# Stage one of batches 1 to 3: the folded transform's two halves as two column tiles of the array, one copy per bank

## The chip, the cores and the metric

The kernel runs on one core of one Trainium2 chip. The metric is device time in microseconds of one execution. The time before is the median of three runs. All durations below come from one profiled execution of the kernel before.

## What is computed

A long convolution by FFT, gated with x, and then a feed-forward block with a squared ReLU, in single precision:

```python
def _attn_ref(x, v, pos_emb, w1, w2):          # x, v: 4 x 12480 x 128
    h_mlp = np.maximum(pos_emb @ w1, 0.0) @ w2
    h_filt = h_mlp * np.exp(-0.01 * np.arange(S))[:, None]
    u = x * v
    Uf = np.fft.rfft(u, n=2 * S, axis=1)
    Hf = np.fft.rfft(h_filt, n=2 * S, axis=0)
    y = np.fft.irfft(Uf * Hf[None], n=2 * S, axis=1)[:, :S, :]
    return x * y

def _moe_ref(x, w_in, w_out):                  # d_ff = 2048
    h = np.maximum(x @ w_in, 0.0)
    return h * h @ w_out
```

## The kernel before, in words

Each batch has 112 x 112 (padded) positions and 128 channels. Its FFT convolution goes through four stages, each a generator: `stage1` (transform along one index of the 112 x 112 grid), `stage2` (twiddles, second transform, product with the filter's spectrum `Hd`), `stage3` and `stage4` (the way back, and the product with x). The first batch's stages and the filter's run at the start of the kernel by themselves. After that the feed-forward block runs over 4 x 28 column groups `i` of 446 columns, each in 8 steps `f`. Between its pieces a step of that loop takes up the next pieces of the FFT stages of batches 1 to 3: `adv(1)`, `adv(2)` and `adv(3)` each run the generator chain up to its next `yield`. One feed-forward step so carries one iteration of the stage that is due: its loads and evacuation (1), its preparation (2) and its matmuls (3). The instructions of each engine are in the order in which Python emits them.

On TensorE a feed-forward step is twelve matmuls of 128 x 128 weights with 446 columns (lines 81 to 83: six into `A`, six into `O` or, late in the kernel, `F`). They are of type float32r. Stage one of batches 1 to 3 uses plain float32: `matmul` at line 297.

`stage1` with `big=False` has 32 iterations `t` (four channels each). `mul(t)` on GpSimd forms x times v, and from it `ut`: for each channel, 112 rows (the index that is summed over), columns 0 to 55 with the sum of two halves of the sequence, columns 56 to 63 zero, columns 64 to 119 with their difference. `mm(t)` takes two PSUM banks `A[h]` and for each of two channels `k` in a bank runs one matmul: `ut`'s 120 columns are the weights, the table `ef` (112 x 224, cosine and minus sine interleaved) streams through. Sums come out on PSUM partitions 0 to 55, differences on 64 to 119.

The difference rows need the table times -i: real and imaginary part exchanged, one of them negated. `evac(t, A)`, which runs one iteration later, does this on the way to `W`. For bank `h = 0`, ScalarE makes three instructions (line 316 for partitions 0 to 63, lines 317 and 318 for the two parts of partitions 64 to 119). For `h = 1`, VectorE makes two (line 309, and line 310 with the factors of the small tile `sign`). `ef` is loaded from `e_full` on the SP queue at the head of the stage, ahead of the first loads of x and v (lines 255 and 256); GpSimd writes `sign` by two memsets there.

The tag `F` has three PSUM banks. The matmul helper `mm3` (lines 81 to 83) is shared by all float32r matmuls.

Of the kernel before, what the change touches and what calls it, by code (L numbers as in the profile page):

```python
# [7 lines left out]
F32 = mybir.dt.float32  # L8
# [9 lines left out]
I = 112  # L18
# [12 lines left out]
HI = I // 2  # L31
KP = 64 + HI
# [3 lines left out]
def hyena_moe_kernel(  # L36
# [22 lines left out]
    nc = tc.nc  # L59
# [12 lines left out]
    def pool(name, side="left", **kw):  # L72
        return tc.tile_pool(name=name, bufs=kw.pop("bufs", 2), side=side, reuse_waits="tile", **kw)

    def bank():
        return psf.tile([128, 512], F32, tag="F", name="F")

    def mm3(o, L, R, first=True, last=True):
        lh, ll = L
        rh, rl = R  # L80
        nc.tensor.matmul(o, lh, rh, start=first, stop=False)  # L81
        nc.tensor.matmul(o, lh, rl, start=False, stop=False)  # L82
        nc.tensor.matmul(o, ll, rh, start=False, stop=last)  # L83
# [54 lines left out]
    def by_value():  # L138
        return W[:I].rearrange("p t (c d) -> p (t c) d", c=4)
# [4 lines left out]
    def first_rows():  # L144
        return W[:I].rearrange("p t (q d) -> p (t q) d", q=4)[:, :I].rearrange("p (e s) (c k) -> p c e s k", e=4, k=4)
# [77 lines left out]
    def rest(k):  # L223
        for _ in range(k):
            yield 1
            yield 2
            yield 3

    def stage1(b, big, et=None, side="left", hook=None):
        DC = 4  # L230
        n = D // DC
        with pool("s1", side) as p:
            if big:
                E = (et[:, 0, :], et[:, 1, :])
            else:
                ef = p.tile([I, 2 * I], F32, name="ef", bufs=1)
                nc.sync.dma_start(out=ef, in_=e_full)
                sign = p.tile([KP, 2], F32, name="sign", bufs=1)
                nc.gpsimd.memset(sign[:, 0:1], 1.0)
                nc.gpsimd.memset(sign[:, 1:2], -1.0)  # L240
            ext = 3 if big else 0
            pa = (3 if b is None else 2) if big else 1
            fold = not big
            J = KP if fold else I
            L = {}
            halves = [p.tile([I, DC, KP], F32, name=f"ut{k}", bufs=1) for k in range(3)] if fold else []
            for ut in halves:
                nc.gpsimd.memset(ut[:, :, HI:64], 0.0)

            def load(t):  # L250
                if b is None or t >= n:
                    return
                xt = p.tile([I, DC, I], F32, tag="xt", name="xt", bufs=2 + pa + ext)
                vt = p.tile([I, DC, I], F32, tag="vt", name="vt", bufs=2 + ext)
                nc.sync.dma_start(out=xt, in_=xs[b, :, t * DC : (t + 1) * DC, :])
                nc.sync.dma_start(out=vt, in_=vs[b, :, t * DC : (t + 1) * DC, :])
                L[t] = xt, vt

            def mul(t):
                if b is None or t >= n:  # L260
                    return
                xt, vt = L[t]
                eng = nc.vector if big and t in (0, 2, 4) else nc.gpsimd
                eng.tensor_mul(out=xt, in0=xt, in1=vt)
                if fold:
                    ut = halves[t % 3]
                    eng.tensor_add(out=ut[:, :, :HI], in0=xt[:, :, :HI], in1=xt[:, :, HI:])
                    eng.tensor_sub(out=ut[:, :, 64:], in0=xt[:, :, :HI], in1=xt[:, :, HI:])
                    L[t] = ut, None

            def like(x):
                return x if b is not None else x.rearrange("p d (s k) -> p d s k", k=4)

            def prep(t):
                if t >= n or fold:
                    return
                u = first_rows()[:, t] if b is None else L.pop(t)[0]
                hi = p.tile([I, DC, J], F32R, tag="uh", name="uh", bufs=1 + pa)
                nc.scalar.copy(like(hi), u)
                q[t] = u, hi  # L280

            def prep2(t):
                if t >= n or fold:
                    return
                u, hi = q[t]
                lo = p.tile([I, DC, J], F32R, tag="ul", name="ul", bufs=1 + pa)
                nc.vector.tensor_sub(out=like(lo), in0=u, in1=like(hi).bitcast(F32))
                q[t] = hi, lo

            def mm(t):  # L290
                hi, lo = (L.pop(t)[0], None) if fold else q.pop(t)
                A = []
                for h in range(DC // 2):
                    A.append(bank())
                    for k in range(2):
                        if fold:
                            nc.tensor.matmul(A[h][:J, k * 2 * I : (k + 1) * 2 * I], hi[:, 2 * h + k, :], ef, start=True, stop=True)  # L297
                            continue
                        mm3(A[h][:J, k * 2 * I : (k + 1) * 2 * I], (hi[:, 2 * h + k, :], lo[:, 2 * h + k, :]), E)
                return A  # L300

            def evac(t, A):
                for h in range(DC // 2):
                    d0 = t * DC + 2 * h
                    if fold:
                        view = W.rearrange("p t (k r d) -> p (t k) r d", k=2, r=2)[:, :, :, d0 : d0 + 2]
                        src = A[h][:KP, : 4 * I].rearrange("p (d c r) -> p c r d", d=2, r=2)
                        if h:
                            nc.vector.tensor_copy(view[:64], src[:64])
                            nc.vector.tensor_mul(  # L310
                                out=view[64:],
                                in0=src[64:, :, ::-1],
                                in1=sign[64:].rearrange("p (c r d) -> p c r d", c=1, d=1).to_broadcast([HI, I, 2, 2]),
                            )
                        else:
                            nc.scalar.copy(view[:64], src[:64])
                            nc.scalar.copy(view[64:, :, 0], src[64:, :, 1])
                            nc.scalar.mul(view[64:, :, 1], src[64:, :, 0], -1.0)
                        continue
                    dst = by_value()[:, :, d0 : d0 + 2]  # L320
                    src = A[h][:I, : 4 * I].rearrange("p (d t) -> p t d", d=2)
                    if big and h:
                        nc.vector.tensor_copy(dst, src)
                    else:
                        nc.scalar.copy(dst, src)

            q = {}
            la = 2 + pa + ext
            early = min(la, 2 + ext)
            for t in range(early):  # L330
                load(t)
            if big:
                yield 1
            else:
                yield from rest(2)
            for t in range(pa + 1):
                mul(t)
            for t in range(early, la):
                load(t)
            yield 1  # L340
            for t in range(pa):
                prep(t)
            yield 2
            for t in range(pa):
                prep2(t)
            prev = None
            for t in range(n):
                yield 1
                load(t + la)
                mul(t + pa + 1)  # L350
                if prev is not None:
                    evac(t - 1, prev)
                prep(t + pa)
                yield 2
                prep2(t + pa)
                yield 3
                prev = mm(t)
                if hook is not None:
                    hook(t - n)
            yield 1  # L360
            evac(n - 1, prev)
# [515 lines left out]
    for i in range(B * NG):  # L877
        for f in range(NS):
            adv(1)
            A = m_h(zT, f)  # L880
# [24 lines left out]
def _constants():  # L905
# [7 lines left out]
    def split(a):  # L913
        hi = r12(a)
        return hi, r12(a - hi.astype(np.float64))

    def split16(a):
        hi = a.astype(np.float16)
        return hi, (a - hi.astype(np.float64)).astype(np.float16)
# [2 lines left out]
    m = np.arange(NP)  # L922
    a = 2 * np.pi * ((4 * n[None] + 1) * n[:, None] % (4 * I)) / (4 * I)
    e = np.stack([np.cos(a), -np.sin(a)], 2).reshape(I, 2 * I)
    e_full = e.astype(np.float32)
    e_tab = np.stack(split(e), 1)

    def th(i):
# [7 lines left out]
    k = n[:, None] + I * n[None]  # L936
# [4 lines left out]
    c, s = split16(np.cos(ph)), split16(np.sin(ph))  # L941
    t2 = np.stack([c[0], s[0], c[1], s[1]], 2)
    ph = angle(2 * n - (I - 1))
    c, s = split16(np.cos(ph)), split16(np.sin(ph))
# [8 lines left out]
    c, s = split16(np.cos(ph)), split16(np.sin(ph))  # L953
# [69 lines left out]
```

## Time and profile before

| what | value |
|---|---|
| median of 3 runs | 3316.22 us (3314.28 to 3319.64) |
| the profiled execution's own time | 3318.15 us |
| its span, first to last instruction | 3316.4 us |
| mean granted TensorE clock | 0.994 of full speed |

The span is 1.75 us less than the profiled execution's time. In the rows below PE is TensorE's matmuls, PEld its weight loads, DVE VectorE, ACT ScalarE, POOL GpSimd, SP the queue that issues most transfers. One float32 `matmul` statement shows as two weight loads and two matmul records; a float32r one as one of each. A matmul record's duration reaches to its modelled end, so records of one engine overlap; the distance from start to start is the time that it occupies.

### The profile page before, as it was taken

To read this page: it belongs to the slowest core of one execution; us is meant where nothing else is said; L and a number is where in the kernel's file an instruction comes from. 1 tells how busy PE (TensorE), PEld (TensorE's weight loads), DVE (VectorE), ACT (ScalarE), POOL (GpSimd) and SP (SyncE) were. 2 spreads that over 40 slices of the span, in tenths; PEclk is the share of its full clock that TensorE was granted. 3 is DMA by queue.
4 is the path that set the end of the run, shared out by engine and by line. 5 is a ranking of instruction groups with operands and counts; after the bars stand their busy time and mean duration, and the time that the engine had idled before them with its cause. 6 is when DMAs were issued, how large, how long until landed. Compare 5 with 4: busy or idle time off the path is not lost.

```text
span 3316.4 us, 55144 instructions
## 1 busy us (share of the span) xinstructions
PE 3266.2 (98%) x18814; PEld 3046.0 (92%) x18814; DVE 2644.3 (80%) x3330; ACT 2571.5 (78%) x3577; POOL 1336.1 (40%) x1411
## 2 busy tenths in 40 slices
PE   8999999999999999999999999999999999999998
PEld 8987989999999999999999999999999999999998
DVE  7999888878876689888876689888876679877776
ACT  6665778777788878778788788778787878888886
POOL 2579046646710046656620056665630046300000
PEclk9999999999999999999999999999999999999999
DMA  2899156434410056533410046533420046300000
GB/s 80 255 261 256 59 135 156 129 94 121 121 35 18 22 129 158 134 100 112 121 45 18 18 117 157 132 111 107 122 62 12 17 101 158 93 26 24 25 23 20
DMA packets 338627, 321.65 MB, mean 97 GB/s; under 512 B 144873, under 2 KB 295273, under 8 KB 338345
## 3 DMA queue, kind: packets, MB, share of 16 engines
q1 hardware_dynamic: 307368, 260.90, 28.8%
q0 software_dynamic: 30976, 57.22, 7.4%
q8 instruction: 149, 2.44, 0.3%
q14 instruction: 134, 1.09, 0.1%
HBM read 226.53 MB, written 63.77 MB: 88 GB/s over the span
## 4 chain that ended last, share of the span: by engine, by line
PE 93%; DVE 2%; DMA 2%; issue 1%; ACT 1%; POOL 0%; SPq 0%; DVEq 0%; POOLq 0%; ACTq 0%
PE A L81 11%; PE A L83 11%; PE A L82 11%; PE F L81 9%; PE F L82 9%; PE O L82 9%; PE F L83 9%; PE O L83 9%; PE O L81 9%; PE F L297 4%; PE F L462 4%; DMA ht<-Hd 1%; DVE m L482 1%; DVE W L482 0%; DVE gl L822 0%
## 5 line engine op out<-in xcount | busy, mean ns | idle before, releaser
L803 ACT ACTIVATE r<-A 128x892 f32<-128x892 f32 x896 | 820.6, 916 | 302.1 <-PE A L83 284.9
L81 PE MATMUL A<-zh,wt 128*128 128x446 f32 x1792 | 702.0, 392 | 1.3 <-DVE gl L822 1.1
L822 DVE TENSOR_TENSOR gl<-r,gh 128x892 fp32r<-128x892 f32 x503 | 612.7, 1218 | 88.1 <-ACT r L810 74.5
L83 PE MATMUL A<-zh,wt 128*128 128x446 f32 x1792 | 653.5, 365 | 0.0
L82 PE MATMUL A<-zl,wt 128*128 128x446 f32 x1792 | 651.5, 364 | 0.0
L806 ACT ACTIVATE gh<-r 128x892 fp32r<-128x892 f32 x512 | 486.2, 950 | 142.6 <-PE O L83 131.2
L770 POOL TENSOR_TENSOR zl<-zi,zh 128x446 fp32r<-128x446 f32 x111 | 129.9, 1170 | 1150.8 <-PE F L83 600.9
L817 DVE CAST gh<-r 128x892 fp32r<-128x892 f32 x384 | 242.5, 631 | 359.2 <-ACT r L810 357.7
L82 PE MATMUL O<-gl,wt 128*128 128x446 f32 x1440 | 524.0, 364 | 1.5 <-DVE gl L822 1.3
L83 PE MATMUL O<-gh,wt 128*128 128x446 f32 x1440 | 524.2, 364 | 0.0
L81 PE MATMUL O<-gh,wt 128*128 128x446 f32 x1440 | 523.2, 363 | 0.0
L810 ACT ACTIVATE r<-r 128x892 f32<-128x892 f32 x504 | 479.3, 951 | 14.5
L822 DVE TENSOR_TENSOR gl<-A,gh 128x892 fp32r<-128x892 f32 x392 | 426.1, 1087 | 74.0 <-ACT gh L806 56.5
L808 DVE SCALAR_TENSOR_TENSOR A<-A,r 128x892 f32<-128x892 f32 x392 | 425.1, 1085 | 56.1 <-ACT r L803 53.9
L81 PEld LDWEIGHTS A<-zh,wt 128*128 128x128 f32 x1792 | 338.7, 189 | 26.9 <-DVE gl L822 2.4
L82 PEld LDWEIGHTS A<-zl,wt 128*128 128x128 f32 x1792 | 340.2, 190 | 19.8 <-DVE zl L770 0.2
L83 PEld LDWEIGHTS A<-zh,wt 128*128 128x128 f32 x1792 | 336.7, 188 | 22.8
L484 POOL TENSOR_TENSOR W<-W,m 112x256 f32<-112x256 f32 x224 | 230.9, 1031 | 206.4 <-DVE m L482 183.1
L621 POOL TENSOR_TENSOR al<-W,ah 112x512 fp32r<-112x512 f32 x212 | 278.7, 1315 | 47.2 <-ACT ah L619 34.2
L82 PEld LDWEIGHTS O<-gl,wt 128*128 128x128 f32 x1440 | 272.4, 189 | 22.5 <-DVE gl L822 3.3
L81 PEld LDWEIGHTS O<-gh,wt 128*128 128x128 f32 x1440 | 271.7, 189 | 18.8
L83 PEld LDWEIGHTS O<-gh,wt 128*128 128x128 f32 x1440 | 269.9, 187 | 18.2
(130 smaller groups left out, 6908.5 us busy)
## 6 DMA issues: line engine op xcount, KB each, us to landing
ht<-Hd SPq DMA_DIRECT2D x224, 224.0 KB
tb<-t POOLq DMA_DIRECT2D x224, 196.0 KB, 3.3
xt<-xs SPq DMA_DIRECT2D x128, 196.0 KB
vt<-vs SPq DMA_DIRECT2D x128, 196.0 KB
xt<-x SPq DMA_DIRECT2D x224, 112.0 KB
out<-ot SPq DMA_DIRECT2D x112, 223.0 KB
tb<-t2s SPq DMA_DIRECT2D x168, 105.0 KB
zd<-zs SPq DMA_DIRECT2D x222, 64.0 KB
```

The lines of the kernel that those rows point to most:

```text
L81: nc.tensor.matmul(o, lh, rh, start=first, stop=False)
L82: nc.tensor.matmul(o, lh, rl, start=False, stop=False)
L83: nc.tensor.matmul(o, ll, rh, start=False, stop=last)
L297: nc.tensor.matmul(A[h][:J, k * 2 * I : (k + 1) * 2 * I], hi[:, 2 * h + k, :], ef, start=True, stop=True)
L484: nc.gpsimd.tensor_sub(out=re[0], in0=re[0], in1=im[1])
L621: eng.tensor_sub(out=lo, in0=w, in1=hi.bitcast(F32))
L803: nc.scalar.activation(r, h, AF.Relu)
L806: nc.scalar.activation(hi, r, AF.Square)
L808: nc.vector.scalar_tensor_tensor(out=h, in0=h, scalar=0.0, in1=r, op0=ALU.max, op1=ALU.mult)
L810: nc.scalar.activation(r, r, AF.Square)
L817: nc.vector.tensor_copy(hi, g)
L822: nc.vector.tensor_sub(out=lo, in0=g, in1=hi.bitcast(F32))
```

## The change

The table gets a second half, -i times the first. Each matmul of 120 weight columns becomes two: the 64 columns of sums (with their zeros) with the first half into partitions 0 to 63, the 56 columns of differences with the second half into partitions 64 to 119. With exchange and sign already in the table, each bank is evacuated by one copy of 120 partitions: ScalarE for bank 0, VectorE for bank 1. The tile `sign` and its two memsets go.

```diff
-                ef = p.tile([I, 2 * I], F32, name="ef", bufs=1)
+                ef = p.tile([I, 2, 2 * I], F32, name="ef", bufs=1)
                 nc.sync.dma_start(out=ef, in_=e_full)
-                sign = p.tile([KP, 2], F32, name="sign", bufs=1)
-                nc.gpsimd.memset(sign[:, 0:1], 1.0)
-                nc.gpsimd.memset(sign[:, 1:2], -1.0)
...
                         if fold:
-                            nc.tensor.matmul(A[h][:J, k * 2 * I : (k + 1) * 2 * I], hi[:, 2 * h + k, :], ef, start=True, stop=True)
+                            o = A[h][:, k * 2 * I : (k + 1) * 2 * I]
+                            nc.tensor.matmul(o[:64], hi[:, 2 * h + k, :64], ef[:, 0, :], start=True, stop=True)
+                            nc.tensor.matmul(o[64:KP], hi[:, 2 * h + k, 64:], ef[:, 1, :], start=True, stop=True)
                             continue
...
                         src = A[h][:KP, : 4 * I].rearrange("p (d c r) -> p c r d", d=2, r=2)
-                        if h:
-                            nc.vector.tensor_copy(view[:64], src[:64])
-                            nc.vector.tensor_mul(
-                                out=view[64:],
-                                in0=src[64:, :, ::-1],
-                                in1=sign[64:].rearrange("p (c r d) -> p c r d", c=1, d=1).to_broadcast([HI, I, 2, 2]),
-                            )
-                        else:
-                            nc.scalar.copy(view[:64], src[:64])
-                            nc.scalar.copy(view[64:, :, 0], src[64:, :, 1])
-                            nc.scalar.mul(view[64:, :, 1], src[64:, :, 0], -1.0)
+                        (nc.vector.tensor_copy if h else nc.scalar.copy)(view[:KP], src)
                         continue
...
-    e_full = e.astype(np.float32)
+    e_full = np.stack([e, np.stack([-np.sin(a), -np.cos(a)], 2).reshape(I, 2 * I)], 1).astype(np.float32)
```

## Rows read from the trace of the kernel before

**Rows 1.** Page: engine, busy us (share of the span), instructions.

```profile
PE 3266.2 (98%) x18814; PEld 3046.0 (92%) x18814; DVE 2644.3 (80%) x3330; ACT 2571.5 (78%) x3577; POOL 1336.1 (40%) x1411
```

**Rows 2.** The chain that ended last, 600 to 740 us: shares, then start, us, what.

```profile
by line: PE F L297 34.8%; PE A L81 11.2%; PE A L83 11.0%; PE A L82 11.0%; PE O L83 10.8%; PE O L82 10.7%; PE O L81 10.7%; issue 0.0%
...
617.99 1.52 PE F L297 x8
...
633.80 1.51 PE F L297 x8
```

**Rows 3.** Busy time of each engine, batch 1's stage one: window, us, busy (instructions), clock, DMA.

```profile
609.82:737.60 127.78, 127.78 (x647) 120.69 (x648) 106.43 (x128) 98.49 (x170) 79.27 (x97) 1.00 0.37 110
```

**Rows 4.** Timeline of PE, 615 to 645 us: start, us, instructions merged where adjacent.

```profile
617.62 0.37 PE L83 MATMUL O<-gh,wt 128*128 128x446 f32 x1
617.82 1.68 PE L297 MATMUL F<-ef,ut 112*120 112x224 f32 x8
619.18 0.53 PE L81 MATMUL A<-zh,wt 128*128 128x446 f32 x1
619.54 0.37 PE L82 MATMUL A<-zl,wt 128*128 128x446 f32 x1
619.75 0.37 PE L83 MATMUL A<-zh,wt 128*128 128x446 f32 x1
...
621.79 1.68 PE L297 MATMUL F<-ef,ut 112*120 112x224 f32 x8
...
625.73 1.68 PE L297 MATMUL F<-ef,ut 112*120 112x224 f32 x8
```

**Rows 5.** Timeline of PEld, 617.5 to 619.6 us, same columns.

```profile
617.62 1.52 PEld L297 LDWEIGHTS F<-ef,ut 112*120 112x120 f32 x8
```

**Rows 6.** Groups by line, whole span: count, busy us, mean ns, idle before.

```profile
L81 PEld LDWEIGHTS A<-zh,wt 128*128 128x128 f32 x1792 | 338.7, 189 | 26.9 <-DVE gl L822 2.4 <-PE F L83 1.1 <-ACT r L803 1.0
...
L297 PE MATMUL F<-ef,ut 112*120 112x224 f32 x768 | 161.3, 352 | 0.0
...
L297 PEld LDWEIGHTS F<-ef,ut 112*120 112x120 f32 x768 | 140.2, 183 | 8.0 <-POOL ut L268 0.6
L462 PEld LDWEIGHTS F<-W,tb 120*112 120x112 f32 x672 | 117.6, 175 | 20.7
...
L310 DVE TENSOR_TENSOR W<-F,sign 56x448 f32<-56x448 f32 x96 | 60.4, 629 | 1.4
...
L309 DVE COPY W<-F 64x448 f32<-64x448 f32 x96 | 58.2, 606 | 0.0
...
L316 ACT COPY W<-F 64x448 f32<-64x448 f32 x96 | 51.8, 540 | 0.1
...
L323 DVE COPY W<-F 112x448 f32<-112x448 f32 x64 | 39.6, 620 | 5.9 <-PE F L83 3.5
...
L325 ACT COPY W<-F 112x448 f32<-112x448 f32 x64 | 36.1, 564 | 10.6 <-DVE W L323 6.4 <-PE F L83 3.9
L318 ACT ACTIVATE W<-F 56x224 f32<-56x224 f32 x96 | 35.3, 368 | 0.0
L317 ACT COPY W<-F 56x224 f32<-56x224 f32 x96 | 34.7, 362 | 1.1
```

**Rows 7.** Timeline of PE in stage three: first and last of twelve float32r pairs, next.

```profile
1001.78 0.27 PE L81 MATMUL F<-tab,vh 112*112 112x224 f32 x1
...
1002.93 0.27 PE L83 MATMUL F<-tab,vl 112*112 112x224 f32 x1
1003.04 0.37 PE L81 MATMUL A<-zh,wt 128*128 128x446 f32 x1
```

**Rows 8.** Who waited for whom, 609 to 738 us: total us, times, longest.

```profile
ACT r L803 <- PE A L83: 18.1, 33, 0.7
POOL ut L267 <- PE F L297: 16.1, 12, 1.6
...
PEld F L297 <- POOL ut L268: 0.4, 1, 0.4
```

**Rows 9.** Timeline of POOL at the head of batch 1's stage one.

```profile
602.50 0.10 POOL L239 MEMSET sign<- 120x1 f32 x1
...
607.23 1.16 POOL L264 TENSOR_TENSOR xt<-xt,vt 112x448 f32<-112x448 f32 x1 [4.43 <-DMA vt<-vs]
```

**Rows 10.** DMA issues: tile, queue, count, KB each; and GB/s in 40 slices.

```profile
GB/s 80 255 261 256 59 135 156 129 94 121 121 35 18 22 129 158 134 100 112 121 45 18 18 117 157 132 111 107 122 62 12 17 101 158 93 26 24 25 23 20
...
ef<-e_full SPq DMA_DIRECT2D x3, 98.0 KB
```

## The prediction

> **What bounds the kernel now.** I read the page's table of engines first: TensorE is busy for 98% of the span, VectorE 80%, ScalarE 78%, GpSimd 40% [rows 1]. That is an average, so the next view is the chain that ended last, cut to batch 1's stage one, where the change sits. There the chain is TensorE's matmuls and nothing else, and line 297 holds 34.8% of it, in pieces of 1.52 us per iteration [rows 2]. The busy times of the same stretch say the same: TensorE 127.78 of 127.78 us, at the full granted clock, with VectorE at 106 and ScalarE at 98 [rows 3]. The waits of the stretch confirm who is late: ScalarE waits for matmuls (18.1 us in all), GpSimd waits for line 297 to release `ut` (16.1 us); TensorE waited once, 0.4 us [rows 8]. So here a microsecond on TensorE is a microsecond of the kernel, and one taken from ScalarE or VectorE is worth nothing until TensorE waits for them.
>
> One iteration on TensorE: from one block of line 297 to the next 3.97 and 3.94 us [rows 4]. Twelve feed-forward matmuls take 0.20 each, 2.4 us; the rest is line 297's eight passes (four statements, two records each). From 617.82 to the next matmul's real start (619.54 less 0.20, since the 0.53 of the record at 619.18 contains the wait for line 297) is 1.52 us, 0.19 per pass. A pass's own record is 352 ns long [rows 6]: its results are still arriving 0.16 us after the next pass has begun. The weight loads (183 ns) lie under the pass ahead: their block begins 0.20 us ahead of the matmuls' [rows 4, 5]. Three batches of 32 iterations make 96 x 1.52 = 146 us of the kernel.
>
> **Evacuation.** ScalarE loses 540 + 362 + 368 = 1270 ns per iteration and gains one copy of 120 x 448. Nearest row: 112 x 448 in 564 ns (line 325). Saved: 0.71 us, 68 us over 96. VectorE: 606 + 629 = 1235 ns become one copy, nearest row 620 ns (line 323): 0.62 us, 59 us over 96 [rows 6]. On the path this is worth between nothing (TensorE never waits for it) and the 0.03 us by which the longer of the two iterations above exceeds the shorter, 96 x 0.03 = 3 us if all of that came from evacuations crossing the matmuls. I take nothing: the matmuls hide both the old and the new copies. If that cover went, 0.7 us per iteration would be the price, but it would have to be a far shorter TensorE block than any below.
>
> **Head of the stage.** Two memsets of 0.10 us leave GpSimd, which then waits 4.43 us for the first `vt` anyway [rows 9]: nothing. The table's transfer grows from 98 to about 196 KB, three times, in front of the first loads of x and v on the same queue. At the 156 GB/s moved in that slice of the span [rows 10] 98 KB are 0.63 us; if all of it delays the first product, 1.9 us in three batches, and nothing if the engines have room. TensorE's idle time behind this chain is 0.6 us in the whole kernel [rows 6], so the cover is thin. I take 1 us.
>
> **The matmuls.** This term decides. Each statement of 120 columns becomes one of 64 and one of 56, each with its own 224 columns streaming: sixteen passes of 0.19 us per iteration where there were eight, and sixteen weight loads. A pass costs by its streamed columns, and these don't shrink. The trace of before has no two matmuls running side by side, so the cost is bounded:
>
> - Lowest: every pass runs beside one of the other half. Eight times 0.19, no change.
> - Highest: the halves run one after another. Sixteen passes, 3.04 us, +1.52 us per iteration, +146 us.
>
> Between them, what can overlap follows from the order of issue. Each statement is two passes on the same half (its weights are loaded twice, rows of line 297), and matmuls start in program order everywhere in the timeline. The first half's two passes come first, and the second of them must wait for the first. The second half's first pass is behind both, so it can start with the first half's second pass; its own second pass then runs beside the next channel's first. So after one lone pass everything goes in pairs, and at the end of the block one lone pass is left: nine times 0.19, 1.71 us, +0.19 per iteration. The issue rate allows that and hardly more: twelve pairs of load and matmul in stage three take 1.26 us, 0.105 each [rows 7], and sixteen at that rate are 1.68 us. Against the highest bound I take the overlap, since the two halves share neither columns of the array nor partitions of the bank.
>
> Next, the joins: into the halves and back to the whole array, twice per iteration. The nearest row, from 120 columns to 128, shows nothing: 0.20 us from the last pass's end to the next start [rows 4]. That is the lower end, but there the array stays one piece. Going between a whole and two halves it may have to be empty, and then each join costs the tail by which a record outlasts its pass, 0.352 - 0.19 = 0.16 us: 0.32 per iteration, 31 us. I take this upper end, since the row with nothing is of a join that changes no division.
>
> The Trainium skill has this as a rule: "TensorEngine Tiling (Array Packing)", section "Key Properties", says that tiles work in parallel and that changing the mode, unlike changing the tile, drains the engine. No row here shows either. By the drain the iteration is 0.19 + 0.32 longer, by the join in the trace 0.19. Its page "TensorE: Matmul & The Clock Gate", section "Measured speedup vs the span model", has three column tiles at 2.38 times; by that efficiency of 0.79, an estimate, eight passes would become 1.92 us, +0.40 per iteration, +38 us.
>
> Weight loads: 189 ns for 128 columns, 183 for 120, 175 for 112 [rows 6]; on that line 64 columns take about 133 ns. Hidden under a pass as today, they cost nothing. Exposed at each change of half, eight times per iteration, they cost 8 x 0.133 = 1.06 us, 102 us in all. I take nothing, as for all loads of line 297 now.
>
> **Sum.** Per iteration +0.19 and +0.32; over 96, +18 and +31; table +1: +50 us. 3318.15 + 50 = 3368; this execution lay 1.9 us above the median of the runs shown, so 3366 us against 3316.22.
>
> **Rivals.**
>
> - *The halves run one after another.* For it: nothing in the trace overlaps in this way; each start waits for the stream ahead. Against it: separate columns, separate partitions. +146 us, 3463; with both joins drained 3493. Chance 0.22, of which 0.08 with the drains.
> - *Overlap, joins free.* For it: the join from 120 to 128 columns. +18 + 1, 3335. Chance 0.18.
> - *Overlap, but a half's weights can't be loaded ahead past the waiting matmul of the other half.* For it: every load in the timeline starts only when the matmul ahead of it has. +18 + 102, 3437. Chance 0.08.
> - *Not slower.* The second half starts beside the first half's first pass, and the lone last pass runs under the next block's start, so that the block stays at 1.52 us; then the quieter evacuation may give the 3 us back. 3313 to 3317. For it: the loads and matmuls have places of their own. Against it: program order. It decides where the block stays under 1.59 us (0.07 x 96 = 6.6 us). Chance 0.16: 0.12 within 0.2%, 0.04 faster by more, which would need a gain on TensorE that no row offers.
>
> **How the numbers follow.** A measurement of this kernel tells differences over about 0.2%, 6.6 us. My forecast (overlap, one lone pass, joins drained in part or whole) has 0.36, and the rivals 0.22, 0.18, 0.08 and 0.16. Slower by over 0.2%: 0.84; within: 0.12; faster: 0.04. The range runs from 3320, which leaves out most of the not slower cases, to 3470, which holds the serial halves without drains; left out are about 0.12 below and 0.08 above.
>
> **What would show it.** In the profile after: records of line 297 doubled to 1536, in two forms of 64 and 56 columns. If they overlap, second-half passes start within a few ns of first-half ones, and the block from its first start to the next feed-forward matmul's real start is near 2.0 us (1.7 without drains, 1.5 for no change, 3.0 if serial). A drain shows at the joins: more than 0.20 us between the last feed-forward start and the block's first, and a gap after its last. Exposed loads show as weight loads of some 130 ns with no matmul starting beside them. ScalarE and VectorE lose some 68 and 59 us of busy time whatever happens, and wait more for TensorE. The prediction is wrong if the block is not longer, if the halves never run side by side, or if TensorE in this stage comes to wait for something other than itself.

## The result, and the profile after

The changed kernel takes 3347.12 us (median of four runs) against 3317.43 us for the kernel before: 29.7 us more, ratio 1.009 with a 95% interval of 1.0073 to 1.0108, which is 24 to 36 us. Four executions in the runs below, at a granted clock of 0.56 to 0.85, took 16% to 62% longer and are left out of the medians and ratios.

The table of engines of the changed kernel's page, to set beside [rows 1]:

```profile
PE 3296.0 (99%) x19582; PEld 2994.6 (90%) x19582; DVE 2590.8 (77%) x3234; ACT 2514.0 (75%) x3385; POOL 1333.1 (40%) x1405
```

TensorE is busy 30 us longer, and so is the span (3345.7 us); ScalarE and VectorE are busy 57 and 54 us less. The busy times of batch 1's stage one (window, us, busy and instructions, clock, DMA share, GB/s) show the same as [rows 3]: TensorE never idle, at the full granted clock, while the relief of the other two is there and unused. The window holds 30 iterations here and 32 in [rows 3], since an iteration has become longer.

```profile
609.45:737.60 128.15, 128.15 (x840) 96.09 (x840) 81.30 (x90) 73.54 (x98) 79.61 (x98) 1.00 0.36 108
```

What the two engines no longer do they wait. The waits of 609 to 738 us (who waited for whom, total us, times, longest), beside [rows 8]; ScalarE's wait for the feed-forward matmuls was 18.1 us there, and VectorE's for ScalarE 11.1 us:

```profile
ACT r L792 <- PE A L83: 44.5, 31, 1.6
DVE A L797 <- ACT r L792: 39.2, 30, 1.7
```

The groups of the changed lines (count, busy us, mean ns, idle before) answer to those of lines 297 and 309 to 318 in [rows 6]. The copies took 557 and 615 ns, where the rows of 112 partitions had promised 564 and 620; by these lines ScalarE sheds 122 - 54 = 68 us and VectorE 119 - 59 = 60, as summed. The page's totals fall by less, 57 and 54: ScalarE's records overlapped each other by 11 us more before, and VectorE's other records have grown by 6.

```profile
L295 PE MATMUL F<-ef,ut 112*64 112x224 f32 x768 | 165.9, 359 | 0.0
L296 PE MATMUL F<-ef,ut 112*56 112x224 f32 x768 | 165.3, 358 | 0.0
L295 PEld LDWEIGHTS F<-ef,ut 112*64 112x64 f32 x768 | 97.3, 136 | 59.8 <-issue 20.0 <-POOL xt L261 5.6 <-POOL ut L264 3.1
...
L307 DVE COPY W<-F 120x448 f32<-120x448 f32 x96 | 59.1, 615 | 0.0
L307 ACT COPY W<-F 120x448 f32<-120x448 f32 x96 | 53.5, 557 | 0.3 <-POOL xt L261 0.3
```

The time is in one iteration's block. Timeline of TensorE's matmuls in the changed kernel (start, us, instruction), beside [rows 4]:

```profile
622.28 0.37 PE L83 MATMUL O<-gh,wt 128*128 128x446 f32 x1
622.58 0.40 PE L295 MATMUL F<-ef,ut 112*64 112x224 f32 x1
622.59 0.40 PE L296 MATMUL F<-ef,ut 112*56 112x224 f32 x1
622.82 0.35 PE L295 MATMUL F<-ef,ut 112*64 112x224 f32 x1
622.82 0.35 PE L296 MATMUL F<-ef,ut 112*56 112x224 f32 x1
...
623.96 0.35 PE L295 MATMUL F<-ef,ut 112*64 112x224 f32 x1
623.96 0.35 PE L296 MATMUL F<-ef,ut 112*56 112x224 f32 x1
624.24 0.47 PE L81 MATMUL A<-zh,wt 128*128 128x446 f32 x1
624.54 0.36 PE L82 MATMUL A<-zl,wt 128*128 128x446 f32 x1
...
626.85 0.40 PE L295 MATMUL F<-ef,ut 112*64 112x224 f32 x1
```

The two halves run in step from the first pass to the last: eight pairs of passes, 0.19 us apart, no lone pass. The whole block, from the end of the feed-forward stream before (622.28 + 0.20) to the real start of the one behind (624.54 - 0.20), is 1.86 us where it was 1.52. Nothing is lost inside. Going in, the first pass really starts at 622.82 - 0.19 = 622.63, 0.15 late; coming out, the last ends at 623.96 + 0.19 = 624.15 and the next starts at 624.34, 0.19 late. An iteration is 4.27 us (622.58 to 626.85) where it was 3.94 or 3.97; the mean distance from block to block in the three stages is 4.27 us, and was 3.95. None of this shows as idle time: the modelled ends of the records reach over both gaps, so TensorE counts as busy in them.

What fills those two gaps stands in the weight loads of the same stretch:

```profile
622.08 0.19 PEld L83 LDWEIGHTS O<-gh,wt 128*128 128x128 f32 x1
622.58 0.13 PEld L295 LDWEIGHTS F<-ef,ut 112*64 112x64 f32 x1 [0.31 <-issue]
622.59 0.13 PEld L296 LDWEIGHTS F<-ef,ut 112*56 112x56 f32 x1
622.63 0.14 PEld L295 LDWEIGHTS F<-ef,ut 112*64 112x64 f32 x1
...
624.24 0.19 PEld L81 LDWEIGHTS A<-zh,wt 128*128 128x128 f32 x1 [0.33 <-issue]
624.35 0.19 PEld L82 LDWEIGHTS A<-zl,wt 128*128 128x128 f32 x1
```

Everywhere else a load starts with the matmul ahead of it and is hidden under it. At a change of division it starts only 0.10 us after the stream ahead has ended (622.58 against 622.48; 624.24 against 624.15), and then the pass has to follow the load: 0.05 us for 64 columns, 0.10 for 128. These two waits bear no semaphore ("issue"): 0.10 + 0.05 going in, 0.09 + 0.10 coming out. From 609 to 738 us all 30 waits on the way out are put down to issue; of the 31 on the way in 20 are, and 11 to GpSimd, but all 31 are about 0.3 us long, whichever it is.

### The profile page after: what moved, and what is told of

It is laid out like the page before. It is cut to its first block, busy times and chain, and to the rows that moved or that the text cites. A ratio compares the mean times of both kernels' runs of the same rounds, so it can differ in the third digit from the quotient of the medians.

```text
span 3345.7 us, 56295 instructions
## 1 busy us (share of the span) xinstructions
PE 3296.0 (99%) x19582; PEld 2994.6 (90%) x19582; DVE 2590.8 (77%) x3234; ACT 2514.0 (75%) x3385; POOL 1333.1 (40%) x1405
## 4 chain that ended last, share of the span: by engine, by line
PE 94%; DVE 2%; DMA 1%; issue 1%; ACT 1%; POOL 0%; SPq 0%; DVEq 0%; POOLq 0%; ACTq 0%
PE A L81 11%; PE A L83 11%; PE A L82 11%; PE F L81 9%; PE F L82 9%; PE F L83 9%; PE O L82 9%; PE O L83 9%; PE O L81 9%; PE F L295 5%; PE F L451 4%; DMA tb<-t2b 1%; DVE m L471 1%; DVE W L471 0%; DVE gl L811 0%
```

## The experiments

In these, theory J is that the cost is the changes of division alone; the rivals are that the passes themselves are dearer (P), or that the copies give something back (C). Each run is compared with the kernel before, run beside it on the same chip.

**Tiles alone.** The kernel before, with the split matmuls and the old evacuation:

```diff
-nc.tensor.matmul(A[h][:J, k * 2 * I : (k + 1) * 2 * I], hi[:, 2 * h + k, :], ef, start=True, stop=True)
+o = A[h][:, k * 2 * I : (k + 1) * 2 * I]
+nc.tensor.matmul(o[:64], hi[:, 2 * h + k, :64], ef, start=True, stop=True)
+nc.tensor.matmul(o[64:KP], hi[:, 2 * h + k, 64:], ef, start=True, stop=True)
```

> The kernel before with its two halves as column tiles on one and the same table, evacuated as before (five instructions, sign on the way). Theory J (each change between whole array and halves costs about 0.15 us going in and 0.19 us coming out, and the passes themselves cost nothing): 96 x 0.34 = +33 us over the kernel before, about 3350. Rival C (the copies give back a few us of the cost in the changed kernel): 2 to 4 us slower than the changed kernel's +30. Both can hold at once; if the time is the changed kernel's within 2 us, the copies gave nothing back.

Measured: 3349.16 us against 3317.20, +32.0, ratio 1.0099 (1.0085 to 1.0113). The whole slowdown is in the tiles: it is that of the changed kernel to within about 2 us, less than the intervals can tell apart.

**Copies alone.** The old matmuls with `(nc.vector.tensor_copy if h else nc.scalar.copy)(view[:KP], src)`:

> The kernel before with its whole-array matmuls, but one plain copy per bank: it leaves out the multiplication of the difference rows by -i, so batches 1 to 3 hold other values. TensorE as before. Theory J with TensorE as the only bound: no difference (within 3 us), ScalarE about 68 and VectorE about 59 us less busy. Rival C: 2 to 4 us faster.

Measured: 3317.37 against 3317.20, ratio 0.9999 (0.9990 to 1.0008). In the stretch 615 to 735 us VectorE and ScalarE fall to 82 and 74 us (in the kernel before 101 and 93), TensorE stays at 120 of 120; the kernel before first, then this run:

```profile
615.00:735.00 120.00, 120.00 (x609) 113.36 (x609) 101.47 (x122) 92.58 (x161) 74.25 (x91) 1.00 0.36 107
615.00:735.00 120.00, 120.00 (x609) 113.36 (x608) 81.83 (x91) 73.61 (x99) 77.12 (x95) 1.00 0.38 112
```

Taking a fifth of their work in this stage from two engines was worth nothing that can be measured. Rival C's 2 to 4 us are not seen; the interval reaches to 3 us. The traces are finer: from block to block both have 3.94, 3.94 and 3.97 us in turn, 3.95 on average, so the 0.03 us of the longer iterations don't come from the evacuations either.

**Half the tiled passes, the same changes.** Bank 0 split, bank 1 whole: `if h == 0:` ahead of the two matmuls, the old one under `else:`.

> As tiles_only, but bank 0 alone in column tiles, bank 1 with the whole array: half the tiled passes, as many changes of division (one in, one out per iteration). Theory J: the same as tiles_only, +30 to +35 us. Rival P (a tiled pass is dearer than a whole one, by a sixteenth of 0.34 us each): half, +16 us.

Measured: 3349.77, +32.6, ratio 1.0099 (1.0085 to 1.0113): the same as with all passes tiled. Rival P falls.

**Half the tiled passes, twice the changes.** The same with `if k == 0:`, so that split and whole statements alternate.

> As tiles_only, but in each bank the first channel in column tiles and the second with the whole array: half the tiled passes, twice the changes of division (two in, two out per iteration). Theory J: about +66 us, 3383. Rival P: half of tiles_only, +16 us.

Measured: 3380.51, +63.3, ratio 1.0196 (1.0182 to 1.0210), twice the cost. Its timeline shows the same gaps between two float32 blocks, so they don't hang on the feed-forward matmuls or their type:

```profile
624.31 0.35 PE L299 MATMUL F<-ef,ut 112*64 112x224 f32 x1
624.31 0.35 PE L300 MATMUL F<-ef,ut 112*56 112x224 f32 x1
624.59 0.64 PE L302 MATMUL F<-ef,ut 112*120 112x224 f32 x2
625.16 0.40 PE L299 MATMUL F<-ef,ut 112*64 112x224 f32 x1
625.17 0.40 PE L300 MATMUL F<-ef,ut 112*56 112x224 f32 x1
625.40 0.35 PE L299 MATMUL F<-ef,ut 112*64 112x224 f32 x1
```

From 624.31 to 625.40 there are four passes, 0.76 us by their streams; the other 0.33 are one change out and one in.

**Half the changes.** Split only in even iterations, `if t % 2 == 0:`.

> As tiles_only, but only the even iterations in column tiles, the odd ones with the whole array: half the tiled passes and half the changes of division of tiles_only. Theory J: +16 us over the kernel before, 3333. Together with one_bank (half the passes, all the changes, +32) this parts changes from passes. Rival P: +16 as well.

Measured: 3333.11 against 3317.93, +15.2, ratio 1.0042 (1.0029 to 1.0055). As many tiled passes as in the two runs before; 1, 2 and 4 changes per iteration on average give 15, 33 and 63 us. That settles theory J: 0.16 to 0.17 us for each.

**Why no lone pass.** The prediction had taken that the second half waits for the first half's second pass, by program order. The changed kernel with the eight statements of an iteration regrouped:

```diff
-for h in range(DC // 2):
-    A.append(bank())
-    for k in range(2):
-        o = A[h][:, k * 2 * I : (k + 1) * 2 * I]
-        nc.tensor.matmul(o[:64], hi[:, 2 * h + k, :64], ef[:, 0, :], start=True, stop=True)
-        nc.tensor.matmul(o[64:KP], hi[:, 2 * h + k, 64:], ef[:, 1, :], start=True, stop=True)
+A = [bank() for h in range(DC // 2)]
+for part in range(2):
+    for c in range(DC):
+        o = A[c // 2][:, c % 2 * 2 * I : (c % 2 + 1) * 2 * I]
+        s = slice(64, KP) if part else slice(0, 64)
+        nc.tensor.matmul(o[s], hi[:, c, s], ef[:, part, :], start=True, stop=True)
```

> The changed kernel, but an iteration issues the four statements of the first half and then the four of the second. Theory O (statements start in program order, and only neighbours on different halves run side by side): six passes alone, two beside each other, six alone, so 14 passes of 0.189 us for 8, +1.13 us per iteration, +109 us over the changed kernel, 3456. Rival Q (each half takes its statements independently of the other): no difference from the changed kernel, 3347. The prediction's lone pass rested on theory O with two passes of a statement in a row.

Measured: 3424.25, +106.3 over the kernel before, ratio 1.0317 (1.0297 to 1.0336), and 77 over the changed one: between the two theories. Its timeline has the block from 626.42 + 0.20 to 629.50 - 0.20, 2.68 us, 0.82 longer than the changed kernel's 1.86:

```profile
626.42 0.37 PE L83 MATMUL O<-gh,wt 128*128 128x446 f32 x1
626.72 2.53 PE L296 MATMUL F<-ef,ut 112*64 112x224 f32 x16
629.19 0.47 PE L81 MATMUL A<-zh,wt 128*128 128x446 f32 x1
629.50 0.36 PE L82 MATMUL A<-zl,wt 128*128 128x446 f32 x1
```

The weight loads by shape say where: in 626.90 to 627.50 only those of the first half, in 627.70 to 628.28 both, in 628.42 to 628.85 only those of the second:

```profile
L296 PEld LDWEIGHTS F<-ef,ut 112*64 112x64 f32 x4 | 0.5, 137 | 0.2
```

```profile
L296 PEld LDWEIGHTS F<-ef,ut 112*56 112x56 f32 x4 | 0.5, 130 | 0.1
L296 PEld LDWEIGHTS F<-ef,ut 112*64 112x64 f32 x2 | 0.3, 137 | 0.0
```

```profile
L296 PEld LDWEIGHTS F<-ef,ut 112*56 112x56 f32 x3 | 0.4, 130 | 0.2
```

Four passes ran alone at each end and four beside each other: twelve places for eight, 4 x 0.19 = 0.76 of the 0.82 us. So a half whose turn comes later in the program starts before the other half's queued passes are done, but not at once: here the second half began when the first had four of its eight passes still to stream. It is no wait for GpSimd's `ut`, since the second half starts 0.81 us after the first in all 96 blocks, whenever `ut` was done. Nor is it the rate of issue, since the next run puts out thirty-two passes in less time than these sixteen took. It fits an engine that looks only some passes ahead; that is a reading, and no run varies the depth. With the change's alternation by two passes such a reach is enough, and the lone pass is gone.

**Four tiles.** Slices of 32, 32, 32 and 24 columns on one table:

```diff
+for c in range(0, KP, 32):
+    s = slice(c, min(c + 32, KP))
+    nc.tensor.matmul(o[s], hi[:, 2 * h + k, s], ef, start=True, stop=True)
```

> As tiles_only, but four column tiles of 32, 32, 32 and 24 columns on the same table. If all four run side by side: eight passes per iteration as before, and the change into tiles is dearer by the empty wait and one load of 32 columns in place of 64 (0.027 us instead of 0.053 by the starts in the changed kernel's trace), so 2 to 3 us faster than tiles_only, 3346. If only two run at a time: 146 us slower than tiles_only.

Measured: 3347.67, +29.7, ratio 1.0084 (1.0069 to 1.0098). Thirty-two passes take the place of eight:

```profile
622.59 0.37 PE L83 MATMUL O<-gh,wt 128*128 128x446 f32 x1
622.88 1.71 PE L300 MATMUL F<-ef,ut 112*32 112x224 f32 x32
624.53 0.47 PE L81 MATMUL A<-zh,wt 128*128 128x446 f32 x1
624.84 0.36 PE L82 MATMUL A<-zl,wt 128*128 128x446 f32 x1
```

The block is 624.64 less 622.79, 1.85 us: all four run side by side. The shorter first load can't be told apart at this accuracy.

**The other way round.** If only TensorE counts in this stage and the others have room, their time should buy passes. Stage one's four float32 statements (eight passes of 0.189) become twelve float32r products on the whole array, as batch 0 has them, with rounding and remainder made by the other engines:

```diff
+hi = p.tile([I, DC, KP], F32R, tag="uh", name="uh", bufs=2)
+nc.scalar.copy(hi, u)
...
+for e, s in ((nc.vector, slice(0, 2)), (nc.gpsimd, slice(2, 4))):
+    e.tensor_sub(out=lo[:, s], in0=u[:, s], in1=hi[:, s].bitcast(F32))
...
-nc.tensor.matmul(A[h][:J, k * 2 * I : (k + 1) * 2 * I], hi[:, 2 * h + k, :], ef, start=True, stop=True)
+mm3(A[h][:J, k * 2 * I : (k + 1) * 2 * I], (hi[:, 2 * h + k, :], lo[:, 2 * h + k, :]), E)
```

> The other way round: ScalarE, VectorE and GpSimd do more so that TensorE does less. The kernel before with stage one's four float32 statements (8 passes of 0.189 us) replaced by twelve float32r ones on the whole array (0.105 each by stage three's rows), evacuated as before. ScalarE rounds the 112 x 480 block (about 0.57 us), VectorE and GpSimd take half each of the remainder. Theory J with TensorE as the only bound: 1.52 - 1.26 = 0.26 us per iteration, 96 x 0.26 = 25 us faster than before, 3292. Rival B (VectorE or ScalarE becomes the bound at 3.6 of 3.7 us per iteration): 0 to 10 us faster, or slower.

Measured: 3340.78, +22.8, ratio 1.0067 (1.0054 to 1.0080): rival B, on its slower side. From 615 to 735 us TensorE's weight loads wait 24 times for VectorE (who waited for whom, total us, times, longest):

```profile
PEld A L81 <- DVE gl L832: 7.3, 24, 0.7
```

Most iterations take 3.9 to 4.0 us where 3.69 had been promised, and about three in ten 4.3 or more. In one of the long ones VectorE's timeline has no gap from 660.49 to 664.94, 4.45 us:

```profile
660.49 1.10 DVE L818 SCALAR_TENSOR_TENSOR A<-A,r 128x892 f32<-128x892 f32 x1
661.69 1.09 DVE L832 TENSOR_TENSOR gl<-A,gh 128x892 fp32r<-128x892 f32 x1
662.70 0.61 DVE L319 COPY W<-F 64x448 f32<-64x448 f32 x1
663.32 0.63 DVE L320 TENSOR_TENSOR W<-F,sign 56x448 f32<-56x448 f32 x1
663.98 0.93 DVE L296 TENSOR_TENSOR ul<-ut,uh 112x240 fp32r<-112x240 f32 x1
664.94 1.10 DVE L818 SCALAR_TENSOR_TENSOR A<-A,r 128x892 f32<-128x892 f32 x1
```

The next two leave VectorE as it was: only two, or three, of the four channels go as products, with the whole remainder on GpSimd (shown for two):

```diff
+nc.scalar.copy(hi, u[:, :2])
...
+nc.gpsimd.tensor_sub(out=lo, in0=u[:, :2], in1=hi.bitcast(F32))
...
-if fold:
+if 2 * h + k >= 2 and fold:
```

> As three_products, but only two of the four channels go as float32r products (the rounding of 240 columns on ScalarE, the remainder on GpSimd alone, VectorE as in the kernel before); the other two stay float32 on the whole array. Theory J with TensorE as the only bound: 4 x 0.189 - 6 x 0.105 = 0.13 us per iteration less, 12 us faster than before, 3305; VectorE at 3.3, ScalarE at 3.4 and GpSimd at 3.3 us of 3.82 stay under it. Rival B (engines near the bound cost more than their sums, as in three_products): no faster, or slower.

> As two_of_four with three channels: 0.19 us per iteration less on TensorE, 18 us faster, 3299, if TensorE stays the bound; GpSimd then comes to 3.65 of 3.76 us, so rival B (GpSimd is late with the remainder) has its place here: less gain than two_of_four, or a loss.

Measured: 3321.02 and 3321.88 against 3317.66, both ratios 1.0016 (1.0007, 1.0006 to 1.0025). The iterations do get shorter (two_of_four: mostly 3.80 and 3.84 us), but the head of the stage loses what they bring. Matmuls of two_of_four at the head of batch 1, the idle time ahead of them and its releaser in brackets:

```profile
608.08 0.36 PE L83 MATMUL O<-gh,wt 128*128 128x446 f32 x1
609.51 0.36 PE L81 MATMUL F<-er,uh 112*120 112x224 f32 x1 [1.06 <-ACT uh L283]
...
612.19 0.54 PE L83 MATMUL F<-er,ul 112*120 112x224 f32 x1 [2.21 <-POOL ul L297]
...
613.13 1.71 PE L311 MATMUL F<-ef,ut 112*120 112x224 f32 x4
...
618.04 0.92 PE L311 MATMUL F<-ef,ut 112*120 112x224 f32 x4
```

TensorE stands for 3.3 us behind the first rounding and the first remainder, which wait for GpSimd's first products. Then it runs at half speed: after this stretch with little work the granted clock is 0.50, the lower of the two levels (1.2 GHz), and four passes take 1.71 us at 613.13 where they take 0.92 at 618.04. Busy times of 612 to 615 us, clock third from the end:

```profile
612.00:615.00 3.00, 2.81 (x9) 2.59 (x10) 2.73 (x4) 2.93 (x6) 2.92 (x5) 0.50 0.45 128
```

The other two heads show the same fall, and by the granted clock each loses about 1.6 us to it. With 2.2 to 3.3 us of waiting that makes some 13 us in three heads, which uses up the 93 x 0.13 = 12 us that the shorter iterations bring; a few late iterations come on top. In the next two runs there are two more feed-forward steps in between:

```diff
             for t in range(early, la):
                 load(t)
+            if fold:
+                yield from rest(2)
             yield 1
```

> two_of_four, whose iterations are 0.13 us shorter but which loses about 4 us at the head of each batch's stage one (TensorE waits for the first rounding and remainder behind the first loads), with two more feed-forward steps between the first products and the first rounding. If that wait is what ate the gain: 3 x 4 us back, about 9 us faster than the kernel before, 3308 to 3310. If the engines' load itself is the matter: as two_of_four, +3 us.

> three_of_four with the same two steps. Its steady iterations are 0.19 us shorter, but some of them take 0.4 to 0.7 us more, where the remainder on GpSimd is late. If the head's wait is what counts: 10 to 14 us faster than before, 3304 to 3308. If GpSimd's late iterations count: no better than two_later.

Measured: 3311.50 and 3310.49 against 3316.65, ratios 0.9985 (0.9976 to 0.9994) and 0.9982 (0.9974 to 0.9991): 5 and 6 us faster than the kernel before, and so faster than the changed one too. That is less than the 9 and 10 to 14 expected. In two_later the granted clock stays at 1.00 at the three heads. The 18 us of the shorter iterations don't arrive in three_later; it is no better than two_later within the intervals, as the late remainders on GpSimd would have it. Its trace bears that out: 72 of the 93 distances from block to block are 3.74 to 3.79 us, but 21 are 4.1 to 5.5. Just as often, 11.9 us in all, weight loads wait for the remainder (in two_later 6 times, 3.1 us). In batch 1:

```profile
PEld F L83 <- POOL ul L297: 4.9, 8, 1.7
```

So the late remainders are most of what is missing. No run has the feed-forward matmuls as halves too, which would leave no change of division.

## Why the prediction held, point by point

*TensorE is the only bound, and the copies are worth nothing.* Shown to within 3 us by the copies alone (0.9999), and by the unchanged distance from block to block in their trace.

*The halves overlap, so the passes cost little.* Right, and better than assumed. The step that failed is the lone pass: "The second half's first pass is behind both, so it can start with the first half's second pass". The halves start within 0.01 us of each other, and the term of +18 us is zero. The order does count, but only when the halves stand far apart in the program: regrouped, it costs 77 us. Sharing the array costs the pairs nothing: 0.19 us each, as a single pass took before, where one estimate of the prediction had +0.40 us per iteration. Nor are 0.105 us for a load and its matmul a limit of issue, as the prediction read [rows 7]: sixteen passes took 1.52 us, 0.095 each, and the four tiles' thirty-two no longer.

*The joins.* Forecast 0.32 us per iteration, 31 us; found 0.34, which is 33 us over 96; by the mean distance from block to block, 4.27 - 3.95, it is 0.32 and 31. The size was right and the reason half right. It isn't the whole 0.16 us by which a record outlasts its pass: the array stands for 0.10 us after the stream ahead, and then a weight load that is hidden everywhere else lies open, 0.05 or 0.10 us. The Trainium skill's rule ("TensorEngine Tiling (Array Packing)", section "Key Properties": a change of mode drains, a change of tile doesn't) agrees with this trace in that a change of division waits, 0.15 us in and 0.19 us out, and a change of half doesn't. Whether the array is empty before the load starts the trace can't show, since the ends of its records are modelled.

*Exposed loads.* That rival saw the right mechanism in the wrong place: no load is exposed between the halves, one is at each join.

*The head.* The table's extra 98 KB were to cost 1 us. That can't be read off the start of the first block, 609.45 us in batch 1 against 609.82: with the old table that start lies anywhere from 605.8 (four_tiles) to 612.9 us (copies_only). In the trace TensorE is idle for at most 0.15 us at each of the three heads, as before, and the first iteration is 0.3 us longer than the rest in batch 1 alone (0.1 before), so a cost of 1 us isn't seen. The working had the wrong slice as well: the table is loaded at 602, 1356 and 2113 us, in slices with 129, 134 and 132 GB/s and not 156, so its upper bound was 2.2 us and not 1.9.

So the sum of +50 us was 20 too high, nearly all of it the lone pass. The rival with the joins free (3335 us) lies nearer to the 3347 us measured than the forecast (3366), but by accident: it had the one term that wasn't there and not the one that was. The serial halves and the unchanged block are excluded by the timeline.

## What to carry to other kernels

Column tiles of float32 cost TensorE nothing inside a block here, also with different tables, as long as the halves alternate closely in the program; every change between the whole array and tiles cost about 0.15 to 0.2 us, so count the changes and not the tiles, and don't sprinkle small tiled blocks between whole-array ones in a stage that TensorE bounds. Before work is taken off an engine, look whether anybody waits for it: here two engines shed a fifth of theirs in this stage for nothing. Giving them more to do for fewer passes did pay, once the head of the stage had the lead for it, but less than half of what the passes alone promised: with GpSimd's sum close to the iteration's length its remainder came late in about a quarter of the iterations of three_later. And a wait of TensorE can cost more than its length: behind the heads of two_of_four the clock was at its lower level.

## What the runs showed of the hardware that I had not expected

- A later statement on another column tile overtakes the queued passes of an earlier one: the second half starts 0.01 us after the first though the first has a second pass to run. In the regrouped kernel it starts with four of the first half's eight passes still to stream.
- Four column tiles run 32 passes of 224 columns in the time of eight, a block of 1.85 us with both joins.
- In three_products VectorE's remainder of 112 x 240 took 0.93 us in the iteration shown and 0.59 in the one before; why wasn't looked into.
- In two_of_four TensorE ran two matmuls between 608.3 and 612.2 us, and its granted clock was 0.50 until past 615 us, which cost another 1.6 us; all three heads show the fall.
